# Gate logits of a routed expert layer from 32-column float32 tiles, once per unit of two head pairs

## The chip, the cores and the metric

The kernel runs on one core of a Trainium2 chip. The metric is the device time of one execution in microseconds (us); the time before is the median of three runs. The engines are TensorE (PE in the profile, PEld for its weight loads), VectorE (DVE), ScalarE (ACT), GpSimd (POOL) and SyncE (SP, which issues most DMA transfers).

## The reference

Sigmoid attention over 8 batches, 12 heads, 448 tokens and 64 elements a head, and behind it a layer of 8 experts of which each token uses one:

```python
scores = scale * np.matmul(q, k.transpose(0, 1, 3, 2)) - np.log(S)
attn = 1.0 / (1.0 + np.exp(-scores))
x = np.matmul(attn, v)                     # heads side by side: (8 * 448, 768)
logits = x @ w_gate                        # (3584, 8)
expert_idx = np.argmax(logits, axis=1)
probs = softmax(logits)                    # with 1e-09 under the line
gate_w = probs[np.arange(N), expert_idx]
for e in range(E):                         # xe: the tokens of expert e
    out[mask] = gate_w[mask, None] * (np.maximum(xe @ w1[e], 0.0) @ w2[e])
```

The gate's logits are a small product: 768 inputs and 8 outputs for each token. They decide which expert's weights are loaded, so they stand between the attention of a batch and its expert products.

## The kernel before

**Tiles.** A pair is two heads of one batch (128 rows); there are 48 pairs, 6 to a batch, and a unit is two pairs, so a batch has three units. A unit's attention runs in seven steps. `scores` (line 534) makes the score products of a step in the four 64x64 quarters of TensorE, `squash` (line 521) takes the sigmoid on ScalarE into a tile `at` of a ring of eight, and `weighted` (line 548) multiplies by the values into PSUM, `av`. All of this is in float32, of which each product shows as two records in the profile.

**When a unit's last values are made** (from line 551), ScalarE writes the product rounded to float32r, `xh` (line 556), VectorE writes the rest, `xl` (line 557), and `token_block` transposes the pair on VectorE into `xt` (line 411), which goes out to the table of tokens. The expert products of `moe` (lines 218 and 237) read `xh` and `xl`: each product is made from three float32r products, high by high, high by low and low by high, of 448 columns. `part_split` (lines 143 and 144) splits the weights in the same way, the high part on ScalarE and the low one on VectorE.

**The gate.** `gate_a` runs once per batch: twelve products (line 265), of `xh` and of `xl` of each pair, with `wgs`, the gate's weights as a high and a low half of eight columns each, add up in one PSUM tile of 16 rows; VectorE copies it into `g16`. `gate_b` turns `g16` into rows of tokens with four transpositions (line 274) and adds the halves. Then `gate_c`, `gate_d` and `gate_e` choose the experts, count the tokens and spread the gate weights.

**The order** is written by hand in `attention` (from line 576), a generator. Its step number is `s`, its unit `u` and the place in the unit `i`. Up to step 35 (`ALONE`) each step has one step of scores and, two steps back, one of values; behind that the seven steps of a unit run as one block at `i` = 6. From step 36 (`START`) the generator hands out 7 expert products at each of its two yields. Between the yields stand the loads and turns of the next unit's k and q (`READY`) and one piece of the gate of the batch whose last unit is done. On each engine the instructions run in the order in which they are written. So there is a lead-in with attention alone, in which the first batch's gate lies, then a long stretch in which expert products and blocks of attention take turns, then a last stage for the tokens that were not sent to their batch's most frequent expert (lines 677 to the end; `few_rows`, line 903, works in tiles of 32 columns, and `split_rows`, line 800, transposes 128x128 blocks).

Of the kernel before, what the change touches and what calls it, by code (L numbers as in the profile page):

```python
# [10 lines left out]
F32 = mybir.dt.float32  # L11
F32R = mybir.dt.float32r
# [4 lines left out]
ALU = mybir.AluOpType  # L17
AX = mybir.AxisListType

P = 128  # L20
NCH = 4
# [4 lines left out]
def tile_sigmoid_attention_top1_moe(  # L26
# [18 lines left out]
    nc = tc.nc  # L45
    B, H, S, D = q.shape
    NT, DM = out.shape
    E = w_gate.shape[1]
    DF = w1.shape[2]
    NP = H // 2  # L50
# [47 lines left out]
    base = const.tile([P, E], F32, name="base")  # L98
    nc.vector.memset(base, 0.0)
    gates = const.tile([P, B, NCH], F32, name="gates")  # L100
    g16 = const.tile([2 * E, NCH * P], F32, name="g16")
    nc.gpsimd.memset(g16, 0.0)

    wgs = const.tile([P, KD, 2 * E], F32R, name="wgs")

    wg = const.tile([P, KD, E], F32, name="wg")

    def setup():
        nc.gpsimd.tensor_copy(wgs[:, :, 0:E], wg)
        nc.gpsimd.tensor_sub(wgs[:, :, E : 2 * E], wg, wgs[:, :, 0:E].bitcast(F32))  # L110
        blank = wpool.tile([P, 1024], U32, tag="wst", bufs=RAWS_AHEAD, name="blank")
        blank3 = blank[:, : E * NT // P * 2].rearrange("p (r w) -> p r w", w=2)
        for w, val in enumerate((int(BIG), 0)):
            nc.gpsimd.iota(blank3[:, :, w], pattern=[[0, E * NT // P]], base=val, channel_multiplier=0)
        nc.gpsimd.dma_start(recs.rearrange("(p r) w -> p r w", p=P), blank3)
# [142 lines left out]
    xch = {}  # L258
    regs = {}

    def gate_a(b):
        psg = small_ps(b, "psg")
        for t in range(KD):
            for n in range(2):
                nc.tensor.matmul(  # L265
                    psg[: 2 * E, :S], wgs[:, t], xch[b, t][n],
                    start=(t == 0 and n == 0), stop=(t == KD - 1 and n == 1),
                )
        nc.vector.tensor_copy(g16[:, :S], psg[: 2 * E, :S])

    def gate_b(b):
        pl = small_ps(b, "pl")
        for c in range(NCH):
            nc.tensor.transpose(  # L274
                pl[:, c * 2 * E : (c + 1) * 2 * E], g16[:, c * P : (c + 1) * P], ident[: 2 * E, : 2 * E]
            )
        plv = pl[:, : NCH * 2 * E].rearrange("p (c n e) -> p c n e", n=2, e=E)
        sh = [P, NCH, E]

        def tl(nm, shape=sh, dt=F32):  # L280
# [3 lines left out]
            return a.unsqueeze(2).broadcast_to(sh)  # L284

        lg = tl("lg")
        nc.vector.tensor_copy(lg, plv[:, :, 0])
        nc.vector.tensor_add(lg, lg, plv[:, :, 1])
        mx = tl("mx", [P, NCH])
        nc.vector.tensor_reduce(mx, lg, axis=AX.X, op=ALU.max)  # L290
        eq = tl("eq")
# [132 lines left out]
    def small_ps(b, name):  # L424

        return ps_sc.tile([P, 512], F32, tag="sc", name=f"{name}_{b}")
# [84 lines left out]
        for _ in range(n):  # L511
            nc.tensor.matmul(ps[:, :P], ones, ones, start=True, stop=True)

    ats, psv = {}, {}

    ST = KC
    N_ST = NG // 2 * ST
# [20 lines left out]
    def weighted(s):  # L538
# [12 lines left out]
        if c == KC - 1:  # L551
            for g in two:
                pv = psv.pop(g)
                xh = xpool.tile([P, S], F32R, tag="xh", name=f"xh_{g}")
                xl = xpool.tile([P, S], F32R, tag="xl", name=f"xl_{g}")
                nc.scalar.copy(xh, pv[:, :S])  # L556
                nc.vector.tensor_sub(xl, pv[:, :S], xh.bitcast(F32))  # L557
                token_block(g, pv[:, :S])
                xch[divmod(g, NP)] = (xh, xl)
# [16 lines left out]
    def attention():  # L576
# [36 lines left out]
        for s in range(N_ST + 11):  # L613
# [11 lines left out]
            yield s, MIX[0]  # L625
            if i in READY and s < N_ST:
                READY[i](u)
            gb = s - PB
            if gb >= 0:
                b, r = divmod(gb, PB)  # L630
                r -= 3 if b == 0 else 2
                at = ("a", "b", None, "c", "l", None) + (("d", None, "e") if b else (None,) * 3 + ("d", "e"))
                what = at[r] if 0 <= r < len(at) else None
                if what == "a":
                    gate_a(b)
                elif what == "b":
                    pend_gate = gate_b(b)
                elif what == "c":
                    pend_gate = gate_c(b, *pend_gate)
# [418 lines left out]
```

## Time and profile before

| | us |
|---|---|
| time, median of 3 runs | 831.76 (830.7 to 833.89) |
| time of the profiled execution | 831.49 |
| its span, first to last instruction | 829.8 |
| TensorE products of line 265, busy | 21.0 in 8 stretches of 2.6 |
| transpositions of line 274, busy | 3.3 |
| copies of psg (line 269), busy on VectorE | 4.9 |

The profile comes from one execution. A timeline row is: start, length, engine, line, operation, output<-inputs by the kernel's names, the part of the array that a product uses (rows*columns), its sizes, how many merged records, and in brackets the idle time of the engine before it with what ended it. A row of a group has the count, then busy time and mean length in ns, then idle time before. TensorE's products are pipelined: one begins before the one ahead of it has ended, so the distance of two starts is what a product costs, and the length of a record is longer than that.

### The profile page before, as it was taken

To read this page: it belongs to the slowest core of one execution; us is meant where nothing else is said; L and a number is where in the kernel's file an instruction comes from. 1 tells how busy PE (TensorE), PEld (TensorE's weight loads), DVE (VectorE), ACT (ScalarE), POOL (GpSimd) and SP (SyncE) were. 2 spreads that over 40 slices of the span, in tenths; PEclk is the share of its full clock that TensorE was granted. 3 is DMA by queue.
4 is the path that set the end of the run, shared out by engine and by line. 5 is a ranking of instruction groups with operands and counts; after the bars stand their busy time and mean duration, and the time that the engine had idled before them with its cause. 6 is when DMAs were issued, how large, how long until landed. Compare 5 with 4: busy or idle time off the path is not lost.

```text
span 829.8 us, 15348 instructions
## 1 busy us (share of the span) xinstructions
PE 814.9 (98%) x5659; PEld 623.4 (75%) x5659; DVE 398.9 (48%) x851; ACT 383.7 (46%) x672; POOL 144.3 (17%) x214
## 2 busy tenths in 40 slices
PE   9999999999999999999999999999999999999994
PEld 6546677687697686786776876876867868999992
DVE  2446365353473264453562534733654535745650
ACT  5766635535534535446344445255363452233440
POOL 3426101210041000410021100400015001512201
PEclk9999999999999999999999999999999999999998
DMA  9999783684575763954758846647635432767921
GB/s 149 141 181 179 203 195 88 142 181 115 138 152 119 180 135 84 211 134 103 169 109 135 202 96 135 154 102 179 126 105 138 134 79 66 185 179 259 325 75 37
DMA packets 290929, 120.70 MB, mean 145 GB/s; under 512 B 204290, under 2 KB 283029, under 8 KB 290848
## 3 DMA queue, kind: packets, MB, share of 16 engines
q1 hardware_dynamic: 279856, 99.27, 52.1%
q0 software_dynamic: 8816, 19.46, 9.4%
q10 hardware_dynamic: 2176, 0.92, 0.8%
q8 instruction: 48, 0.79, 0.4%
q14 instruction: 33, 0.27, 0.1%
HBM read 97.55 MB, written 23.17 MB: 145 GB/s over the span
## 4 chain that ended last, share of the span: by engine, by line
PE 94%; DMA 2%; SPq 2%; issue 1%; POOL 0%; POOLq 0%; DVE 0%; DVEq 0%
PE ps L237 29%; PE ps L218 29%; PE sc L534 15%; PE av L548 14%; PE psg L265 2%; PE ps L881 2%; PE ps L861 2%; SPq L457 1%; DMA kn<-in_k_dram 1%; DMA qn<-in_q_dram 1%; DMA first<-in_k_dram 1%; DMA out_dram<-xo,rec_c 0%; PE pl L274 0%; SPq L497 0%; SPq L471 0%
## 5 line engine op out<-in xcount | busy, mean ns | idle before, releaser
L521 ACT ACTIVATE at<-sc,bias_s 128x448 f32<-128x448 f32 x336 | 196.2, 632 | 135.5 <-PE sc L534 134.3
L534 PE MATMUL sc<-qt,kt 64*64 64x448 f32 x1344 | 175.1, 545 | 1.9 <-DVE qt L505 1.8
L548 PE MATMUL av<-at,vn 64*64 64x448 f32 x1344 | 173.9, 537 | 0.0
L237 PE MATMUL ps<-hh,w2l 128*128 128x448 f32 x384 | 142.1, 370 | 0.0
L253 POOL DMA_DIRECT2D out_dram<-ob x96 | 61.5, 653 | 461.6 <-DVE ob L248 384.6
L237 PE MATMUL ps<-hh,w2h 128*128 128x448 f32 x384 | 141.6, 369 | 0.0
L218 PE MATMUL ps<-xl,w1h 128*128 128x448 f32 x384 | 141.5, 368 | 0.0
L218 PE MATMUL ps<-xh,w1l 128*128 128x448 f32 x384 | 140.9, 367 | 0.0
L237 PE MATMUL ps<-hl,w2h 128*128 128x448 f32 x384 | 140.8, 367 | 0.0
L218 PE MATMUL ps<-xh,w1h 128*128 128x448 f32 x384 | 140.5, 366 | 0.0
L557 DVE TENSOR_TENSOR xl<-av,xh 128x448 fp32r<-128x448 f32 x48 | 29.0, 604 | 216.6 <-ACT xh L556 216.6
L534 PEld LDWEIGHTS sc<-qt,kt 64*64 64x64 f32 x1344 | 79.9, 191 | 60.5 <-issue 25.9
L223 ACT ACTIVATE hh<-ps 128x448 fp32r<-128x448 f32 x64 | 35.0, 547 | 161.8 <-PE ps L218 161.7
L548 PEld LDWEIGHTS av<-at,vn 64*64 64x64 f32 x1344 | 64.0, 132 | 60.2 <-ACT at L521 25.5
L143 ACT CAST w2h<-wst 128x512 fp32r<-128x512 f32 x96 | 61.6, 659 | 87.0 <-PE ps L237 80.4
L218 PEld LDWEIGHTS ps<-xl,w1h 128*128 128x128 f32 x384 | 72.1, 188 | 11.0 <-issue 5.2
L237 PEld LDWEIGHTS ps<-hh,w2h 128*128 128x128 f32 x384 | 72.2, 188 | 9.5 <-issue 4.2
L237 PEld LDWEIGHTS ps<-hh,w2l 128*128 128x128 f32 x384 | 72.2, 188 | 8.4 <-issue 2.8
L218 PEld LDWEIGHTS ps<-xh,w1l 128*128 128x128 f32 x384 | 72.1, 188 | 8.4 <-issue 1.4
L218 PEld LDWEIGHTS ps<-xh,w1h 128*128 128x128 f32 x384 | 72.1, 188 | 6.6 <-ACT at L521 0.7
L237 PEld LDWEIGHTS ps<-hl,w2h 128*128 128x128 f32 x384 | 72.2, 188 | 5.6
L144 DVE TENSOR_TENSOR w2l<-wst,w2h 128x512 fp32r<-128x512 f32 x96 | 64.0, 683 | 22.7 <-ACT w2h L143 21.1
(164 smaller groups left out, 741.6 us busy)
## 6 DMA issues: line engine op xcount, KB each, us to landing
wst<-in_moe_w_dram SPq DMA_DIRECT2D x48, 512.0 KB, 4.5
wst<-in_moe_w_dram SPq DMA_DIRECT2D x56, 384.0 KB, 4.3
x_tok<-xt SPq DMA_DIRECT2D x64, 168.0 KB, 4.2
out_dram<-ob POOLq DMA_DIRECT2D x96, 112.0 KB, 3.2
kn<-in_k_dram SPq DMA_DIRECT2D x184, 56.0 KB, 4.1
qn<-in_q_dram SPq DMA_DIRECT2D x168, 56.0 KB, 3.1
vn<-in_v_dram SPq DMA_DIRECT2D x68, 112.0 KB, 3.8
raw<-in_moe_w_dram SPq DMA_DIRECT2D x12, 512.0 KB, 6.6
```

Source lines behind the costliest of these rows:

```text
L143: nc.scalar.copy(hi, st)
L144: eng.tensor_tensor(lo, st, hi.bitcast(F32), op=ALU.subtract)
L218: nc.tensor.matmul(ps[:, :S], a[:, ws], b_, start=(t == 0 and n == 0), stop=(t == KD - 1 and n == 2))
L223: nc.scalar.activation(hh[:, :S], ps[:, :S], AF.Relu)
L237: nc.tensor.matmul(ps[:, :S], a, b_, start=(j == 0 and n == 0), stop=(j == KF - 1 and n == 2))
L253: nc.gpsimd.dma_start(out[b * S : (b + 1) * S, cols].rearrange("(j r) f -> r j f", r=32), obv[32 * i : 32 * (i + 1)])
L265: nc.tensor.matmul(psg[: 2 * E, :S], wgs[:, t], xch[b, t][n], start=(t == 0 and n == 0), stop=(t == KD - 1 and n == 1),)
L521: nc.scalar.activation(at, ps[:, :S], AF.Sigmoid, bias=bias_s, scale=SCALE)
L534: nc.tensor.matmul(ps[quarter(g, h), :S], ks, ops[g, "q"][OWN[h]], start=True, stop=True)
L548: nc.tensor.matmul(psv[g][OWN[h], :S], ops[g, "v"][rows, c, :], at[rows], start=(c == 0), stop=(c == KC - 1))
L557: nc.vector.tensor_sub(xl, pv[:, :S], xh.bitcast(F32))
L861: nc.tensor.matmul(pss[j], a[:, js], b_, start=(t == 0 and m == 0), stop=(t == KD - 1 and m == 2))
```

## The change

The gate no longer reads `xh` and `xl`. A third copy of each pair's product, `plain`, is kept in float32 in the ring of `at`; VectorE writes it up to step 34, ahead of `xl`, and ScalarE behind it, after `xh`. `gate_unit` runs once per unit, on the unit before, at `i` = 2 between the two yields. It makes four float32 products of 32 columns and 256 tokens, one for each pair and each half of the tokens (tokens 0 to 255 and 192 to 447), each into 32 PSUM rows of its own. The weights are `wgp`: eight columns and 24 of zeros. VectorE copies the first unit's tile into `gsum` and adds the other two. `gate_b` then transposes four blocks of 128x128, and one reduction adds the two pairs' parts. `gate_a` is gone, with its twelve products and its copy.

```diff
-    g16 = const.tile([2 * E, NCH * P], F32, name="g16")
-    nc.gpsimd.memset(g16, 0.0)
-
-    wgs = const.tile([P, KD, 2 * E], F32R, name="wgs")
+    GC, GW = 32, 2 * P
+    gsum = const.tile([P, GW + P // 2], F32, name="gsum")
+    nc.gpsimd.memset(gsum, 0.0)
+
+    wgp = const.tile([P, KD, GC], F32, name="wgp")
+    nc.gpsimd.memset(wgp, 0.0)
...
-        nc.gpsimd.tensor_copy(wgs[:, :, 0:E], wg)
-        nc.gpsimd.tensor_sub(wgs[:, :, E : 2 * E], wg, wgs[:, :, 0:E].bitcast(F32))
+        nc.gpsimd.tensor_copy(wgp[:, :, 0:E], wg)
...
-    def gate_a(b):
-        psg = small_ps(b, "psg")
-        for t in range(KD):
-            for n in range(2):
-                nc.tensor.matmul(
-                    psg[: 2 * E, :S], wgs[:, t], xch[b, t][n],
-                    start=(t == 0 and n == 0), stop=(t == KD - 1 and n == 1),
-                )
-        nc.vector.tensor_copy(g16[:, :S], psg[: 2 * E, :S])
+    def gate_unit(u):
+
+        b, n = divmod(2 * u, NP)
+        psg = small_ps(u, "psg")
+        for m in range(2):
+            x = plain.pop(2 * u + m)
+            for half, at in enumerate((0, S - GW)):
+                rows = slice((2 * m + half) * GC, (2 * m + half + 1) * GC)
+                nc.tensor.matmul(psg[rows, :GW], wgp[:, n + m], x[:, at : at + GW], start=True, stop=True)
+        if n == 0:
+            nc.vector.tensor_copy(gsum[:, :GW], psg[:, :GW])
+        else:
+            nc.vector.tensor_add(gsum[:, :GW], psg[:, :GW], gsum[:, :GW])
 
     def gate_b(b):
         pl = small_ps(b, "pl")
-        for c in range(NCH):
-            nc.tensor.transpose(
-                pl[:, c * 2 * E : (c + 1) * 2 * E], g16[:, c * P : (c + 1) * P], ident[: 2 * E, : 2 * E]
-            )
-        plv = pl[:, : NCH * 2 * E].rearrange("p (c n e) -> p c n e", n=2, e=E)
+        for c, at in enumerate((0, P, 2 * P - (S - GW), 3 * P - (S - GW))):
+            to = c * P - c // 2 * GC
+            nc.tensor.transpose(pl[:, to : to + P], gsum[:, at : at + P], ident)
+        plv = pl.rearrange("p (c n x) -> p c x n", c=NCH, n=2)[:, :, :E]
...
-        nc.vector.tensor_copy(lg, plv[:, :, 0])
-        nc.vector.tensor_add(lg, lg, plv[:, :, 1])
+        nc.vector.tensor_reduce(lg, plv, axis=AX.X, op=ALU.add)
...
+                plain[g] = apool.tile([P, S], F32, tag="at", bufs=8, name=f"plain_{g}")
+                if s < ALONE:
+                    nc.vector.tensor_copy(plain[g], pv[:, :S])
                 nc.scalar.copy(xh, pv[:, :S])
+                if s >= ALONE:
+                    nc.scalar.copy(plain[g], pv[:, :S])
                 nc.vector.tensor_sub(xl, pv[:, :S], xh.bitcast(F32))
                 token_block(g, pv[:, :S])
...
+            if i == 2 and 0 < u <= NG // 2:
+                gate_unit(u - 1)
...
-                at = ("a", "b", None, "c", "l", None) + (("d", None, "e") if b else (None,) * 3 + ("d", "e"))
+                at = (None, "b", None, "c", "l", None) + (("d", None, "e") if b else (None,) * 3 + ("d", "e"))
                 what = at[r] if 0 <= r < len(at) else None
-                if what == "a":
-                    gate_a(b)
-                elif what == "b":
+                if what == "b":
```

On TensorE, in the mixed stretch, the gate of batch 1 stood before in the middle of the expert products of one weight tile (`ps_0_6`, the experts' first layer); the numbers behind the names only tell tiles apart:

```order
L218 MATMUL ps_0_6_1504<-xl_594,w1h_6_1415 128x448
L265 MATMUL psg_1520<-xh_967,wgs 16x448
L265 MATMUL psg_1520<-xl_968,wgs 16x448
L265 MATMUL psg_1520<-xh_973,wgs 16x448
L265 MATMUL psg_1520<-xl_974,wgs 16x448
L265 MATMUL psg_1520<-xh_1134,wgs 16x448
L265 MATMUL psg_1520<-xl_1135,wgs 16x448
L265 MATMUL psg_1520<-xh_1139,wgs 16x448
L265 MATMUL psg_1520<-xl_1140,wgs 16x448
L265 MATMUL psg_1520<-xh_1393,wgs 16x448
L265 MATMUL psg_1520<-xl_1394,wgs 16x448
L265 MATMUL psg_1520<-xh_1398,wgs 16x448
```

At the same place the change has one unit's four products (two rows that stand for two each):

```order
L219 MATMUL ps_0_6_1543<-xh_605,w1h_6_1454 128x448
L219 MATMUL ps_0_6_1543<-xl_606,w1h_6_1454 128x448
L270 MATMUL psg_1559<-plain_1430,wgp 32x256 x2
L270 MATMUL psg_1559<-plain_1437,wgp 32x256 x2
L219 MATMUL ps_0_6_1543<-xh_605,w1l_6_1455 128x448
```

The twelfth old product (of `xl_1399`) and the rest of the weight tile follow behind the first of these pieces. The other two units of the batch have places of their own, 7 and 14 steps earlier, and the transpositions stay one step behind the last unit's place.

On VectorE, in the lead-in, the work on the fourth unit's two pairs (`av_766` and `av_769` before, `av_790` and `av_793` in the change) reads before:

```order
L505 STREAM_TRANSPOSE kt_921<-kn_713 128x448
L557 TENSOR_TENSOR xl_968<-av_766,xh_967 128x448
L411 STREAM_TRANSPOSE xt_0_971<-av_766 128x14x32
L557 TENSOR_TENSOR xl_974<-av_769,xh_973 128x448
L411 STREAM_TRANSPOSE xt_0_971<-av_769 128x14x32
L505 STREAM_TRANSPOSE qt_978<-qn_718 128x448
L505 STREAM_TRANSPOSE kt_1017<-kn_788 128x448
```

and in the change:

```order
L508 STREAM_TRANSPOSE kt_936<-kn_733 128x448
L561 COPY plain_984<-av_790 128x448
L565 TENSOR_TENSOR xl_983<-av_790,xh_982 128x448
L414 STREAM_TRANSPOSE xt_0_988<-av_790 128x14x32
L561 COPY plain_992<-av_793 128x448
L565 TENSOR_TENSOR xl_991<-av_793,xh_990 128x448
L414 STREAM_TRANSPOSE xt_0_988<-av_793 128x14x32
L508 STREAM_TRANSPOSE qt_997<-qn_738 128x448
L272 COPY gsum<-psg_1020 128x256
L508 STREAM_TRANSPOSE kt_1042<-kn_818 128x448
```

Each pair has one copy more, ahead of its `xl`, and the copy into `gsum` stands between the turns of q and k. On TensorE the same unit's products come one step (scores and values) behind the last values of its pairs:

```order
L551 MATMUL av_790<-at_6_886,vn_615 64x448 x2
L551 MATMUL av_793<-at_6_888,vn_686 64x448 x2
L537 MATMUL sc_2_1004<-qt_771,kt_731 64x448 x2
L537 MATMUL sc_2_1005<-qt_842,kt_816 64x448 x2
L551 MATMUL av_1014<-at_0_928,vn_773 64x448 x2
L551 MATMUL av_1017<-at_0_930,vn_844 64x448 x2
L270 MATMUL psg_1020<-plain_984,wgp 32x256 x2
L270 MATMUL psg_1020<-plain_992,wgp 32x256 x2
L537 MATMUL sc_3_1028<-qt_771,kt_731 64x448 x2
```

Nothing stood there before: the values of `av` were followed by the next step's scores.

On VectorE at the start of the mixed stretch, the split of the experts' second weight tile (`w1l_1`) stood before behind four operations of the fifth unit and one turn:

```order
L144 TENSOR_TENSOR w1l_0_1113<-wst_0_951,w1h_0_1112 128x768
L557 TENSOR_TENSOR xl_1135<-av_995,xh_1134 128x448
L411 STREAM_TRANSPOSE xt_0_971<-av_995 128x14x32
L557 TENSOR_TENSOR xl_1140<-av_998,xh_1139 128x448
L411 STREAM_TRANSPOSE xt_1_1143<-av_998 128x14x32
L505 STREAM_TRANSPOSE kt_1145<-kn_923 128x448
L144 TENSOR_TENSOR w1l_1_1158<-wst_1_983,w1h_1_1157 128x768
```

and stands now behind six and the turn:

```order
L145 TENSOR_TENSOR w1l_0_1138<-wst_0_966,w1h_0_1137 128x768
L561 COPY plain_1161<-av_1014 128x448
L565 TENSOR_TENSOR xl_1160<-av_1014,xh_1159 128x448
L414 STREAM_TRANSPOSE xt_0_988<-av_1014 128x14x32
L561 COPY plain_1168<-av_1017 128x448
L565 TENSOR_TENSOR xl_1167<-av_1017,xh_1166 128x448
L414 STREAM_TRANSPOSE xt_1_1172<-av_1017 128x14x32
L508 STREAM_TRANSPOSE kt_1174<-kn_938 128x448
L145 TENSOR_TENSOR w1l_1_1187<-wst_1_1002,w1h_1_1186 128x768
```

More of the change, by code (lines that the diff above doesn't have):

```diff
@@ L512, in warm_up @@
             nc.tensor.matmul(ps[:, :P], ones, ones, start=True, stop=True)
-    ats, psv = {}, {}
+    ats, psv, plain = {}, {}, {}
     ST = KC
```

## The prediction

> **What bounds the kernel now.** I read the engines' busy times, the chain of waits, then the timeline of TensorE around the old gate products. The first shows which engine is full, the second whether its time sets the end.
>
> ```profile
> PE 814.9 (98%) x5659; PEld 623.4 (75%) x5659; DVE 398.9 (48%) x851; ACT 383.7 (46%) x672; POOL 144.3 (17%) x214
> PE 94%; DMA 2%; SPq 2%; issue 1%; POOL 0%; POOLq 0%; DVE 0%; DVEq 0%
> ```
>
> TensorE is busy 98% of the span and holds 94% of the chain. VectorE and ScalarE are half idle. So from where the loads stop setting the pace, a microsecond of TensorE time is a microsecond of the kernel, and work on the other two costs something only where TensorE has to wait for it. The change must be priced on TensorE, in two stretches: the lead-in, where attention runs alone, and the long mixed stretch behind it, from the experts' first product on.
>
> **What goes in the mixed stretch.** The old products and transposes of batch 1 stand among the experts' products:
>
> ```profile
> 108.41 0.36 PE L265 MATMUL psg<-xh,wgs 128*16 128x448 f32 x1
> ...
> 110.86 0.37 PE L218 MATMUL ps<-xh,w1l 128*128 128x448 f32 x1
> 113.50 0.37 PE L218 MATMUL ps<-xh,w1h 128*128 128x448 f32 x1
> 113.80 0.42 PE L274 MATMUL pl<-ident,g 16*128 16x16 f32 x4
> ...
> 114.45 0.36 PE L218 MATMUL ps<-xh,w1l 128*128 128x448 f32 x1
> ```
>
> Twelve products take 110.86 - 108.41 = 2.45 us, 0.204 each, the same step as the experts' own; they come and go without a gap. The four transposes cost 114.45 - 113.50 less two ordinary steps (0.41): 0.54 us. Seven batches (1 to 7) lie in this stretch: **-7 x 2.45 = -17.15 us**.
>
> **What comes there.** Twenty of the 24 units (the fifth on) fall into it, each with four 128*32 products of 256 columns between experts' products. The kernel's end has products of exactly this shape, and the way back to full-width products is seen behind a block of 64*64 attention:
>
> ```profile
> L903 PE MATMUL few<-kept,x_few 128*32 128x256 f32 x48 | 2.8, 381 | 0.0
> 811.46 0.28 PE L881 MATMUL ps<-w2l_r,hr 128*128 128x256 f32 x1
> 811.59 0.28 PE L881 MATMUL ps<-w2h_r,hr 128*128 128x256 f32 x1
> 811.80 2.80 PE L903 MATMUL few<-kept,x_few 128*32 128x256 f32 x48
> 131.45 0.95 PE L548 MATMUL av<-at,vn 64*64 64x448 f32 x8
> 132.33 0.47 PE L237 MATMUL ps<-hh,w2h 128*128 128x448 f32 x1
> 132.64 0.37 PE L237 MATMUL ps<-hl,w2h 128*128 128x448 f32 x1
> ```
>
> The 48 records are 24 float32 products, two records each (six tokens' blocks by four tiles). Four run side by side: 12 groups in 2.80 us, the last one 0.38 long, so (2.80 - 0.38) / 11 = 0.22 us a group. A unit is four products, eight records, two groups: 0.44. Going in costs 0.21 against an ordinary step of 0.13 (811.46 to 811.59): 0.08 to 0.09. Coming back: eight 64*64 records take 0.75 (the prologue's rows below step by that), so the next product was due at 132.20 and began at 132.33 (0.13), and the one behind it came after 0.31 in place of 0.20 (0.11). A visit is 0.44 + 0.09 + 0.24 = 0.77 us: **20 x 0.77 = +15.4**.
>
> That way in and out speaks against the change, and the Trainium skill has a rule on it (TensorEngine Tiling (Array Packing), Key Properties): a change of the tiling mode drains TensorE. The rows agree that a change costs something, 0.33 us a visit. A full drain at both ends would make it more, which is the first rival below; with no cost at all a visit would be 0.44 and the 20 would be 6.6 us cheaper.
>
> The new transposes are 128x128, as the final stage has them:
>
> ```profile
> 761.65 0.36 PE L237 MATMUL ps<-hl,w2h 128*128 128x448 f32 x1
> 761.85 0.60 PE L800 MATMUL px<-ident,xo 128*128 128x128 f32 x4
> ...
> 762.49 0.37 PE L237 MATMUL ps<-hh,w2h 128*128 128x448 f32 x1
> ```
>
> Four cost 762.49 - 761.65 - 0.41 = 0.43 us, less than the narrow ones: **7 x (0.43 - 0.54) = -0.8**. The mixed stretch sums to **-2.5 us**.
>
> **The copies on ScalarE and VectorE there.** ScalarE copies each pair's product a second time (about half of the 0.97 us of two casts, see the row of 98.60 below). I cost this at nothing: TensorE comes to the unit 49 products (seven yields, 10.0 us) after the block. What follows the block on ScalarE shifts by about 0.9 us, and the tightest place is the sixth weight tile:
>
> ```profile
> 101.84 1.80 DVE L144 TENSOR_TENSOR w1l<-wst,w1h 128x768 fp32r<-128x768 f32 x2
> 98.60 0.97 ACT L556 CAST xh<-av 128x448 fp32r<-128x448 f32 x2
> 99.87 1.60 ACT L143 CAST w1h<-wst 128x768 fp32r<-128x768 f32 x2
> ```
>
> VectorE first works off its own four operations of the two pairs and takes up w1l at 101.84, while the first of the two casts from 99.87 on, 1.60 us together, ends near 100.7; 0.9 us later it is still in time. Without that cover each late tile would cost up to 0.9 us. The sums into gsum (256 wide) and one reduction for two small operations hide in VectorE's idle half.
>
> **The lead-in.** Here the old gate of batch 0 disappears:
>
> ```profile
> 49.97 0.95 PE L548 MATMUL av<-at,vn 64*64 64x448 f32 x4
> 50.85 0.37 PE L265 MATMUL psg<-xh,wgs 128*16 128x448 f32 x1
> ...
> 54.25 0.93 PE L548 MATMUL av<-at,vn 64*64 64x448 f32 x8
> 55.11 0.42 PE L274 MATMUL pl<-ident,g 16*128 16x16 f32 x4
> 56.32 0.93 PE L548 MATMUL av<-at,vn 64*64 64x448 f32 x8
> ```
>
> From 49.97 + 0.75 to 54.25 - 0.75: **-2.78 us**, of which 0.34 is the way in and out. The transposes cost 56.32 - 0.75 - 55.00 = 0.57; wide ones would be 0.43 + 0.34 = 0.77: **+0.2**.
>
> Four units fall here, and they **wait**. As the rows of the change show, a unit's products stand one step (scores and values, 1.5 us) behind the last values of that unit, while VectorE makes plain of the first pair, then xl and xt, and only then plain of the second. Around the fourth unit the trace of before has
>
> ```profile
> 61.18 0.93 PE L548 MATMUL av<-at,vn 64*64 64x448 f32 x8
> 61.93 0.93 PE L534 MATMUL sc<-qt,kt 64*64 64x448 f32 x8
> 62.68 0.93 PE L548 MATMUL av<-at,vn 64*64 64x448 f32 x8
> 61.70 0.65 DVE L505 STREAM_TRANSPOSE kt<-kn 128x448 f32<-128x448 f32 x1
> 63.07 0.62 DVE L557 TENSOR_TENSOR xl<-av,xh 128x448 fp32r<-128x448 f32 x1 [0.72 <-ACT xh L556]
> 63.61 0.64 DVE L411 STREAM_TRANSPOSE xt<-av 128x448 f32<-128x448 f32 x1
> 64.17 0.58 DVE L557 TENSOR_TENSOR xl<-av,xh 128x448 fp32r<-128x448 f32 x1
> L269 DVE COPY g<-psg 16x448 f32<-16x448 f32 x8 | 4.9, 612 | 16.9 <-PE psg L265 16.9
> ```
>
> The values end at 62.11. A copy of 448 elements a row takes 0.61. The first fits into the 0.72 us in which VectorE waited for ScalarE's cast, so xl still starts at 63.07; the second takes the place of the xl at 64.17 and ends at 64.78. TensorE stands ready at 62.68 + 0.75 + 0.13 = 63.56: it waits about 1.25 us, with the semaphore 1.3. Queued behind it are the next scores, so ScalarE's sigmoids and all that follows slip too. The bounds are 0 (the copy would have to be 0.6 faster and xl out of the way) and 1.9 (another 0.6 behind a late transposition). I take 1.3, which comes out of the rows. VectorE in turn waits for the unit's products before gsum; behind it stand the turns of the next k and q, wanted only at the next unit's first scores, four steps (6 us) later, so that wait costs nothing. A unit here costs 0.44 + 0.34 + 1.3 = 2.1 us.
>
> The first unit is mostly paid already:
>
> ```profile
> 31.75 0.54 PE L534 MATMUL sc<-qt,kt 64*64 64x448 f32 x2
> 34.11 0.65 PE L534 MATMUL sc<-qt,kt 64*64 64x448 f32 x2 [1.81 <-DVE qt L505]
> ```
>
> TensorE idles here behind a load of q, 34.11 - 31.75 - 0.38 = 2.0 us: the first unit's place lies a few steps ahead of it, so its 2.1 us shrink to 0.1. The other three: 3 x 2.1 = 6.2 (from 0.78 + 1.3): **+6.3** with the first.
>
> The fifth unit's copies lie on VectorE at the start of the experts:
>
> ```profile
> 73.39 0.62 DVE L557 TENSOR_TENSOR xl<-av,xh 128x448 fp32r<-128x448 f32 x1 [1.19 <-ACT xh L556]
> 76.09 0.92 DVE L144 TENSOR_TENSOR w1l<-wst,w1h 128x768 fp32r<-128x768 f32 x1
> 76.68 0.36 PE L218 MATMUL ps<-xl,w1h 128*128 128x448 f32 x1
> 77.06 0.47 PE L218 MATMUL ps<-xh,w1l 128*128 128x448 f32 x1
> ```
>
> TensorE already waits for w1l there (0.38 where a step is 0.20). One copy fits into the 1.19 us of idle time, the other pushes w1l by 0.55: **+0.55**. The lead-in sums to -2.78 + 0.2 + 6.3 + 0.55 = **+4.3 us**.
>
> **The sum.** -2.5 + 4.3 = +1.8 us on the profiled execution's 831.49 us: **833.3 us**. That execution lies 0.27 below the median of the runs shown, 831.76, so it stands for them. A measurement of this kernel can tell some 0.5% (4.2 us) from no change, and +1.8 is inside.
>
> **Rivals.**
> *A full drain at each change of shape (slower).* Price: an experts' record is 0.37 long against a step of 0.20 (0.16 to drain going in), a narrow one 0.38 against 0.22 (0.16 coming out), and a full-width weight load, the mean of the next row, would stand open for its 0.19.
>
> ```profile
> L218 PEld LDWEIGHTS ps<-xh,w1h 128*128 128x128 f32 x384 | 72.1, 188 | 6.6 <-ACT at L521 0.7
> ```
>
> That is 0.51 in place of 0.33 a visit: 23 visits x 0.18 = 4.1 more, **837.4 us**. It decides from 0.43 a visit on (2.4 more in sum, past 0.5%). The rows of 811.80 and 132.33 speak against it; that no row shows a 128*32 group directly followed by full width speaks for it. Chance 0.15, with ScalarE's late casts, which would end on the same side.
> *Cheap visits and no wait (faster).* If the switches cost 0.1 a visit (-5.3) and VectorE were early enough to save half the waits (-2), the time is **826 us**. The idle VectorE speaks for it, the two rows of the switches against. Chance 0.07.
> *Four tiles do the work in a quarter.* The old products were 16 columns wide; were tiles to cut their time by four, 7 x 2.45 would become 4.3 us and with the lead-in unchanged at +4.3 the end is 831.5 - 12.9 - 0.8 + 4.3 = **822 us**. The group's own step, 0.22 for a record of 256 columns in float32 (two records a product) against 0.20 for 448 columns before, speaks against it. The Trainium skill (TensorEngine Tiling, Theoretical Speedup) gives up to four times for 32 columns or fewer; the trace does show four side by side, but float32 takes the gain back. Chance 0.03.
> *The tiles don't overlap*, and the change does not do what it says: eight records of 0.22 in a row, 1.3 us more in each of 23 visits, some **864 us**. Line 903 shows the overlap. Chance 0.02.
> My forecast has 0.73.
>
> **Chances and range.** The forecast's own bounds: the wait 0 to 1.9 for three units (-3.9 to +1.8), and the visit 0.6 to 0.95 for twenty (-3.4 to +3.6). Both ends at once are unlikely; 828.5 to 837.5 leaves out about 2 in 10 and takes in the full drain. Faster by over 0.5%: 0.11 (the two faster rivals and a tail of the forecast); within it: 0.70; slower: 0.19 (the drain, no overlap and the other tail).
>
> **What would show it.** In the new trace: a unit's eight records in about 0.6 us (0.22 + 0.38) and the experts' next steps 0.77 late in sum; gaps of about 1.3 us on TensorE before the second pair's products at three places between 38 and 67 us, released by VectorE's plain; the wait at the second weight tile near 0.7; the transposes at 0.43. It is wrong if ScalarE's copies show up as waits for w1l or w2l behind the blocks, if the first unit moves the 34.11 us start, or if the switches cost other than 0.33.

## The result and the profile after

| | before | changed |
|---|---|---|
| time, us, median | 831.1 (829.78 to 833.89) | 838.7 (837.61 to 840.14) |
| ratio | 1 | 1.0086, 95% interval 1.0072 to 1.01 |
| span of the profiled run, us | 829.8 | 836.5 |

The change makes the kernel slower by 0.9%: 7.6 us where 1.8 were forecast, and 838.7 lies outside the range of 828.5 to 837.5. The engines' busy times hardly tell it. TensorE is still full, and the other two are a little busier with the copies:

```profile
PE 819.5 (98%) x5755; PEld 627.6 (75%) x5755; DVE 407.8 (49%) x869; ACT 400.2 (48%) x710; POOL 143.0 (17%) x214
PE 94%; DVE 2%; issue 1%; DMA 1%; ACT 1%; POOL 0%; POOLq 0%; DVEq 0%
```

The second line is the chain of waits: VectorE had 0% of it before and has 2% now, ScalarE 1%. To see where the time went, I took the starts of the same TensorE instructions in both traces, each counted from the first attention score, and subtracted (the middle column gives the starts in the trace of before, from the start of the span). From the 101st product on, over four fifths of the span, the change gives 3 us back:

| TensorE comes to | before, us | changed minus before, us |
|---|---|---|
| the fifth unit's first scores | 58.81 | +2.00 |
| the experts' first product | 72.72 | +4.99 |
| their 25th product | 77.97 | +8.31 |
| their 101st product | 104.55 | +9.92 |
| the last product of the last expert | 776.95 | +6.95 |
| the end | 829.76 | +7.16 |

**The mixed stretch is as forecast.** A visit in the rows of TensorE (start, duration, line, output and inputs, count):

```profile
181.99 0.37 PE L219 MATMUL ps<-xh,w1l 128*128 128x448 f32 x1
182.29 0.64 PE L270 MATMUL psg<-plain,wgp 128*32 128x256 f32 x8
182.86 0.47 PE L219 MATMUL ps<-xh,w1h 128*128 128x448 f32 x1
183.17 0.36 PE L219 MATMUL ps<-xl,w1h 128*128 128x448 f32 x1
```

From 181.99 to 183.17 are 1.18 us where two ordinary steps take 0.41: the visit costs 0.77, as forecast. All 20 measured in this way sum to 15.6 us (0.77 to 0.78 each, one 0.95), the old products to 17.27, and the seven groups of wide transposes cost 0.44 each where the narrow ones cost 0.54. That is -2.4 us, forecast -2.5.

**The lead-in is not.** Around the fourth unit, at the place that the prediction looked at, ScalarE before shows two casts in one go and the sigmoids behind them:

```profile
62.50 0.97 ACT L556 CAST xh<-av 128x448 fp32r<-128x448 f32 x2
63.34 2.28 ACT L521 ACTIVATE at<-sc,bias_s 128x448 f32<-128x448 f32 x4
```

VectorE, ScalarE and TensorE now show (in brackets the idle time before a row and what ended it):

```profile
63.84 0.59 DVE L561 COPY plain<-av 128x448 f32<-128x448 f32 x1
65.03 0.62 DVE L565 TENSOR_TENSOR xl<-av,xh 128x448 fp32r<-128x448 f32 x1 [0.60 <-ACT xh L562]
65.57 0.64 DVE L414 STREAM_TRANSPOSE xt<-av 128x448 f32<-128x448 f32 x1
66.13 0.58 DVE L561 COPY plain<-av 128x448 f32<-128x448 f32 x1
64.46 0.53 ACT L562 CAST xh<-av 128x448 fp32r<-128x448 f32 x1 [0.29 <-DVE plain L561]
66.75 0.53 ACT L562 CAST xh<-av 128x448 fp32r<-128x448 f32 x1 [1.76 <-DVE plain L561]
67.18 2.46 ACT L524 ACTIVATE at<-sc,bias_s 128x448 f32<-128x448 f32 x4
65.10 0.62 PE L270 MATMUL psg<-plain,wgp 128*32 128x256 f32 x4
66.77 0.62 PE L270 MATMUL psg<-plain,wgp 128*32 128x256 f32 x4 [1.04 <-DVE plain L561]
```

Read the casts first. ScalarE's xh does not start beside VectorE's plain: it waits for it, though both only read av. Before, xh waited for nothing of VectorE's, and both casts ran one behind the other. Now a unit's eight operations stand in one file over two engines: plain, xh, xl, xt, and again. The second cast starts 2.29 us behind the first, and the sigmoids of the next attention steps stand behind it in ScalarE's queue (four at 67.18). TensorE's wait for plain is there as forecast. The view of waits below has only 2.3 us of it in four places, but that counts the idle time behind modelled ends of records; by the starts of the scores, each of the second to fourth units loses 2.30 to 2.44 us at its visit, where 2.1 were forecast.

**The start of the experts is the worst place.** The fifth unit's copies stand ahead of the second weight tile there, and the view of waits and TensorE's rows show:

```profile
PE psg L270 <- DVE plain L561: 2.3, 4, 1.0
PE ps L219 <- DVE w1l L145: 1.2, 1, 1.2
PE ps L219 <- ACT w1h L144: 0.6, 1, 0.6
...
80.56 0.53 ACT L562 CAST xh<-av 128x448 fp32r<-128x448 f32 x1 [1.75 <-DVE plain L561]
80.99 0.83 ACT L144 CAST w1h<-wst 128x768 fp32r<-128x768 f32 x1
81.13 0.62 DVE L565 TENSOR_TENSOR xl<-av,xh 128x448 fp32r<-128x448 f32 x1 [0.60 <-ACT xh L562]
82.76 0.92 DVE L145 TENSOR_TENSOR w1l<-wst,w1h 128x768 fp32r<-128x768 f32 x1
80.88 0.37 PE L219 MATMUL ps<-xh,w1l 128*128 128x448 f32 x1
81.88 0.47 PE L219 MATMUL ps<-xh,w1h 128*128 128x448 f32 x1 [0.63 <-ACT w1h L144]
82.19 0.37 PE L219 MATMUL ps<-xl,w1h 128*128 128x448 f32 x1
83.73 0.47 PE L219 MATMUL ps<-xh,w1l 128*128 128x448 f32 x1 [1.17 <-DVE w1l L145]
```

The late second cast makes w1h late, which stands behind it on ScalarE. It makes VectorE's second xl late too, and behind that stand its transposition, a turn and w1l; the two copies are two operations more ahead of w1l than before (w1h itself had ended at 81.82). TensorE shows steps of 1.00 and 1.54 us where an ordinary one is 0.20, 2.13 us lost where before lost 0.17. Behind them the granted clock falls, as the busy times by stretch show (span, busy of PE, PEld, DVE, ACT, POOL with counts, then the granted clock, the DMA share and GB/s):

```profile
77.00:84.00 7.00, 5.19 (x25) 3.78 (x21) 5.19 (x9) 3.06 (x6) 6.39 (x8) 1.00 0.62 94
85.00:88.40 3.40, 3.40 (x11) 2.99 (x11) 1.49 (x3) 0.00 (x0) 1.12 (x3) 0.51 1.08 348
```

Between 84.70 and 88.40 ten products step by 0.37 instead of 0.20, 1.65 us more. The parts between the experts' first and 101st products sum up: waits 2.13 - 0.17, the visit 0.77, the clock 1.65, and 0.47 of late w1l behind the next block make 4.85 of the 4.93 in the table (9.92 - 4.99). The 0.47 has the same root on the other side: xl, which does not read plain, waits there for ScalarE's plain on the same av, and what stands behind xl on VectorE comes later.

```profile
108.60 0.62 DVE L565 TENSOR_TENSOR xl<-av,xh 128x448 fp32r<-128x448 f32 x1 [13.09 <-ACT plain L564]
```

The theory to test, A: the loss comes from the copies, because two engines that read one av stand behind one another, which delays the casts and what is queued behind them. Its rival B: the loss comes from the visits on TensorE. Every ratio below is to the kernel before, run on the same chip.

### The profile page after: what moved, and what is told of

Its sections match the earlier page's. It is cut to its first block, busy times and chain, and to the rows that moved or that the text cites. A ratio compares the mean times of both kernels' runs of the same rounds, so it can differ in the third digit from the quotient of the medians.

```text
span 836.5 us, 15619 instructions
## 1 busy us (share of the span) xinstructions
PE 819.5 (98%) x5755; PEld 627.6 (75%) x5755; DVE 407.8 (49%) x869; ACT 400.2 (48%) x710; POOL 143.0 (17%) x214
## 4 chain that ended last, share of the span: by engine, by line
PE 94%; DVE 2%; issue 1%; DMA 1%; ACT 1%; POOL 0%; POOLq 0%; DVEq 0%
PE ps L238 29%; PE ps L219 28%; PE sc L537 15%; PE av L551 15%; PE ps L889 2%; PE ps L869 2%; PE psg L270 2%; PE ps_warm L515 1%; DVE plain L561 1%; DVE xt L414 0%; DMA out_dram<-xo,rec_c 0%; PE pl L280 0%; DVE xl L565 0%; ACT xh L562 0%; DMA x_tok<-xt 0%
## 5 line engine op out<-in xcount | busy, mean ns | idle before, releaser
L219 PE MATMUL ps<-xh,w1h 128*128 128x448 f32 x384 | 142.2, 370 | 0.7 <-ACT w1h L144 0.6
```

Source lines behind the costliest of these rows:

```text
L219: nc.tensor.matmul(ps[:, :S], a[:, ws], b_, start=(t == 0 and n == 0), stop=(t == KD - 1 and n == 2))
```

## The experiments

**Copies without the new gate.** The kernel before, its twelve products kept, with the change's copies alone:

```diff
+                plain[g] = apool.tile([P, S], F32, tag="at", bufs=8, name=f"plain_{g}")
+                if s < ALONE:
+                    nc.vector.tensor_copy(plain[g], pv[:, :S])
                 nc.scalar.copy(xh, pv[:, :S])
+                if s >= ALONE:
+                    nc.scalar.copy(plain[g], pv[:, :S])
```

> The kernel before (old twelve products a batch) with the change's copies into plain alone, which nothing reads. Theory A: the copies keep their harm at the experts' start (+3 to +4 us) and in the lead-in that of sigmoids queued behind late casts (0 to +1): 834.5 to 836 against 831.1. Theory B: the copies lie beside TensorE's work and cost nothing, 831.1 within 0.7.

Measured: 837.76 us against 830.13, ratio 1.0089 (1.0075 to 1.0102). The copies alone cost as much as the whole change, more than A had put on them, and B falls. TensorE's waits move from plain to the sigmoids, which shows that ScalarE's queue is what comes late:

```profile
PE sc L534 <- ACT at L521: 3.8, 3, 2.0
PE ps L218 <- DVE w1l L144: 1.2, 1, 1.2
```

**The same copies in another order.** In the lead-in VectorE makes plain behind xl and xt, not ahead of xh:

```diff
-                if s < ALONE:
-                    nc.vector.tensor_copy(plain[g], pv[:, :S])
                 nc.scalar.copy(xh, pv[:, :S])
...
                 token_block(g, pv[:, :S])
+                if s < ALONE:
+                    nc.vector.tensor_copy(plain[g], pv[:, :S])
```

> The run with the copies alone, but in the lead-in VectorE makes plain behind xl and xt, so that xh no longer stands behind it. Theory A1 (the harm is that ScalarE's cast waits for VectorE's copy and the sigmoids behind it come late): the lead-in's +4.6 falls to 1.5 or less, sum 831.5 to 834. Theory A2 (it is the 0.6 us a copy on VectorE, that makes turns and w1l late): the lead-in stays at +4 or more, sum 836 to 838.

Measured: 831.88 against 830.92, 1.0013 (1.0001 to 1.0025). The copies are the same in number, kind and engine, and 6.7 of 7.6 us are gone. ScalarE's rows at the fourth unit, first of the run before this one, then of this one:

```profile
65.59 0.53 ACT L559 CAST xh<-av 128x448 fp32r<-128x448 f32 x1 [0.29 <-DVE plain L558]
67.88 0.53 ACT L559 CAST xh<-av 128x448 fp32r<-128x448 f32 x1 [1.76 <-DVE plain L558]
68.31 2.21 ACT L521 ACTIVATE at<-sc,bias_s 128x448 f32<-128x448 f32 x4
```

```profile
61.67 0.97 ACT L557 CAST xh<-av 128x448 fp32r<-128x448 f32 x2
62.50 1.19 ACT L521 ACTIVATE at<-sc,bias_s 128x448 f32<-128x448 f32 x2
```

The sigmoids start 0.83 us behind the first cast instead of 2.72. At the experts' first product this run stands 0.97 us ahead of before, the other 4.61 behind it. Nor is it the ring of `at`: plain takes its buffers there in both runs. The copy's own time on VectorE (0.6 us) is nearly free in the lead-in, but not at the second weight tile: it still waits 1.07 us for w1l. So of the 1.96 us of waits at the experts' start about half is the two copies' own time ahead of w1l, and not their order.

The Trainium skill (PSUM — Partial Sum Buffer, Terms) says that two engines must not access one bank of PSUM at once, and that reads against reads count. The rows shown agree with it: a reader of an av begins when the other engine's reader ahead of it in the code has ended. The wait is one for a semaphore, which the program as built contains; what the chip would do without it, no run shows.

**The fifth unit alone.** In the changed kernel, ScalarE makes its two copies just ahead of its visit, behind the casts of the weights:

```diff
+                if s == FIFTH:
+                    late.append((g, pv))
...
+                while late:
+                    g, pv = late.pop(0)
+                    nc.scalar.copy(plain[g], pv[:, :S])
                 gate_unit(u - 1)
```

> The changed kernel, with one thing undone at the experts' start: the fifth unit's two copies into plain are made by ScalarE just ahead of its four products, not by VectorE ahead of the casts. Theory A (two engines that read one av stand behind one another, so the late casts make w1h and w1l late, TensorE idles 2.5 us in two pieces and its clock then falls to half for some 3.5 us): both waits of the first expert shrink to the 0.4 us of before, no stretch at a clock of 0.5, and 3 to 4 us less than the changed kernel's 838.7: about 835.2. Theory B (the visits are dear, the start of the experts is not what costs): within 0.7 us of 838.7.

Measured: 835.7 against 830.13, 1.0067 (1.0053 to 1.008). Both waits for weights are gone and the clock stays at 1.00, but a new wait takes part of the gain:

```profile
82.88 1.06 PE L270 MATMUL psg<-plain,wgp 128*32 128x256 f32 x8 [0.95 <-ACT plain L642]
```

By the ratios it is 0.2% (1.6 us) less than the changed kernel, half of what A expected, and not clear of the noise: the changed kernel run a second time, below, has 1.0071. What the trace shows is that the two waits are gone and that the copy came too close ahead of its reader.

**Visits later.** The first four units' visits one step later, then the same with the order of the copies put right and the fifth unit's copies behind the second weight tile's split:

```diff
-            if i == 2 and 0 < u <= NG // 2:
+            if i == (3 if u <= 4 else 2) and 0 < u <= NG // 2:
                 gate_unit(u - 1)
```

and for the second, beside this and plain behind xt, the fifth unit's copies:

```diff
+            if s == START:
+                for g, pv in late:
+                    nc.vector.tensor_copy(plain[g], pv[:, :S])
```

> The changed kernel with the four products of the first four units one attention step (1.5 us) later. Theory A: the waits of TensorE for plain (2.3 us in four pieces) go, so up to 2.3 us less, about 836.5; the first expert's waits and the fallen clock stay, since the fifth unit is not touched. Theory B (visits dear): no change, since all 24 visits are still there: 838.7.

> The changed kernel, with plain still copied from av, but in the lead-in by VectorE behind xl and xt, the first four units' products a step later, and the fifth unit's copies behind the second weight tile's split. Theory A1 (order of the readers): the lead-in falls from +5 to within 2 us of before and the experts' start to within 0.5, so 830 to 832.5 beside 830.1 of before. Theory A2 (VectorE's extra 0.6 us a copy): 834 or more.

Measured: 1.0071 (1.0057 to 1.0084) and 1.0023 (1.0013 to 1.0034). In the first, TensorE's wait for plain is gone, but in its place it waits 2.6 us for sigmoids, since psg takes its buffer from the scores' ring and the sigmoids are late behind the casts:

```profile
PE psg L270 <- ACT at L524: 2.6, 3, 1.2
```

The second keeps waits of 1.9 us for the now later plain, so that its lead-in ends 2.92 us behind before where A1 allowed 2; by the ratio, 832.0 beside the 830.1 of the expectation, it lies in A1's range.

**Where plain comes from.** GpSimd makes plain as xh + xl from SBUF for every unit, so that it reads no av, and the first four units' visits are a step later, as in the runs above:

```diff
-                    nc.vector.tensor_copy(plain[g], pv[:, :S])
...
+                nc.gpsimd.tensor_add(plain[g], xh.bitcast(F32), xl.bitcast(F32))
```

> The changed kernel, with plain made by GpSimd as xh + xl from SBUF, so that nobody but xh, xl and xt reads av, as before the change; the first four units' products one step later. Theory A (the copies from av do the harm, the visits are worth 1 to 3 us): lead-in within 1 us of before, the experts' start as before, mixed stretch -1 to -2.5: 828 to 831 where before has 830.1. Theory B (it is the visits): still 6 us over before, 836. If GpSimd's sums hold up VectorE or its own loads, it comes out between.

Measured: 835.11 against 830.92, 1.0043 (1.0027 to 1.0059), between the two theories. The lead-in is only 1.3 us behind before, as A wants, but at the experts' start the two sums hold up VectorE's subtraction:

```profile
76.67 2.24 POOL L562 TENSOR_TENSOR plain<-xh,xl 128x448 f32<-128x448 f32 x2
76.76 2.98 DVE L145 TENSOR_TENSOR w1l<-wst,w1h 128x768 fp32r<-128x768 f32 x1
80.73 0.93 DVE L145 TENSOR_TENSOR w1l<-wst,w1h 128x768 fp32r<-128x768 f32 x1
```

The same subtraction takes 0.93 us without them and 2.98 beside them, and TensorE waits 2.0 us for it. Behind that wait the granted clock was 0.50 from 80.6 to 84.0 us, so this run too pays for a slower clock. The Trainium skill (SBUF — State Buffer, Who interferes with whom) says that a VectorE instruction with two inputs in SBUF is locked out while a GpSimd instruction reads SBUF. The rows fit such a lock: the sums end at 78.91, 0.93 later is 79.84, and the subtraction ended at 79.74.

**The price of a visit.** Two kernels, for rival B: every product from the fifth unit on twice in one visit, and a visit for each pair:

```diff
-        for m in range(2):
-            x = plain.pop(2 * u + m)
+        xs = [plain.pop(2 * u + m) for m in range(2)]
+        for m in (0, 1, 0, 1) if u >= 4 else (0, 1):
+            x = xs[m]
```

```diff
-                gate_unit(u - 1)
+                if u <= 4:
+                    gate_unit(u - 1)
+                else:
+                    gate_unit(u - 1, (0,))
+                    halves.append(u - 1)
```

> The changed kernel, with the four products of every unit from the fifth on issued twice in one visit (the second time over the same sums). Theory A (a visit costs 0.77: two groups of 0.22 and 0.33 of switching): 20 x 0.44 = 8.8 us more, 847.5. Theory B (a full drain at each switch, and tiles that hardly overlap): 20 x 0.9 to 1.7 = 18 us or more, 857 and over.

> The changed kernel, with each unit's four products from the fifth on in two visits, one for each pair, ten expert products apart. Each visit more costs one way in and out and no product. Theory A (0.33 a visit): 20 x 0.33 = 6.6 us more than the changed kernel, ratio to before about 1.0165; half of the pair's overlap of four tiles may be lost, up to 0.22 a visit, 4.4 more. Theory B (a full drain, 0.51): 10 us more, 1.021. No cost of the switch: no more than 1 us.

Measured: 844.22, 1.0177 (1.0164 to 1.0191), and 851.62, 1.0247 (1.0228 to 1.0265). In the first, a visit takes 1.20 us instead of 0.77, so the four products are 0.43 (forecast 0.44) and going in and out 0.34 (forecast 0.33). In the second the two halves stand three expert products apart (not ten, as the expectation has it), and each half visit takes 0.76 us, as much as a whole one:

```profile
182.71 0.63 PE L272 MATMUL psg<-plain,wgp 128*32 128x256 f32 x4
183.26 0.47 PE L219 MATMUL ps<-xh,w1h 128*128 128x448 f32 x1
183.57 0.37 PE L219 MATMUL ps<-xl,w1h 128*128 128x448 f32 x1
183.78 0.36 PE L219 MATMUL ps<-xh,w1l 128*128 128x448 f32 x1
184.07 0.63 PE L272 MATMUL psg<-plain,wgp 128*32 128x256 f32 x4
```

My expectation of 0.33, up to 0.55, a further visit was too low: four records on two tiles take as long as eight on four (0.63 and 0.64), so a half visit saves no product time at all. By TensorE's rows twenty further visits are some 15 us; by the ratios it is 13.4.

**The order, once more, in the changed kernel.** Since the order decided it with the copies alone, the changed kernel was run with that edit and nothing else:

> The changed kernel with only the order of the readers of av changed: in the lead-in VectorE makes plain behind xl and xt, so ScalarE's xh waits for TensorE alone; visits and their places as changed. Theory A1: of the 7.6 us of the copies alone, 6.4 were the order, so about 6 less than the changed kernel, less what the first four units now wait longer for plain (0.7 each, 2.8): 833 to 836, ratio 1.003 to 1.006. Theory A2 (the order matters only without the gate's visits): 838 to 839, ratio 1.0086.

Measured: 841.79 against 830.78, 1.0127 (1.0105 to 1.015). It is slower still, and both expectations fail. The visits stand where they stood, plain is made last, and so TensorE waits for it:

```profile
PE psg L270 <- DVE plain L566: 8.2, 8, 1.3
...
74.00:76.00 2.00, 2.00 (x16) 0.80 (x12) 0.54 (x2) 1.16 (x2) 0.00 (x0) 0.50 1.10 285
```

The second row is the stretch from 74 to 76 us, with the clock at 0.50 behind these waits; it had fallen once before, from 56.2 us on. So the order is good only where the visits are late enough for it. Two more runs complete the square: the visits of units 1, 2, 4 and 5 a further step later and the fifth unit's copies behind the second weight tile, with plain last and with plain first.

```diff
-            if i == (3 if u <= 4 else 2) and 0 < u <= NG // 2:
+            if 0 < u <= NG // 2 and i == {1: 4, 2: 4, 3: 3, 4: 4, 5: 3}.get(u, 2):
                 gate_unit(u - 1)
```

> The run with plain last, with the products of units 1, 2, 4 and 5 another step later, so that they no longer wait for plain. The 1.9 and 0.7 us of waits before psg shrink to 0.7: about 1.9 less than that run, ratio 1.000 (0.999 to 1.002).

> The run with the visits of the lead-in later still, but with the change's order of the readers in the lead-in (VectorE's plain ahead of ScalarE's xh); the fifth unit's copies stay behind the second weight tile. With the visits out of the way of plain, what differs from that run is the order alone. If the order does the harm by itself: 2 to 5 us more in the lead-in, ratio 1.004 to 1.008. If the order only mattered through what waits for it at the visits and at the experts' start: within 1 us of that run, ratio 1.001 to 1.003.

| ratio to before | plain first, as changed | plain last |
|---|---|---|
| visits as changed | 1.0086 (1.0072 to 1.01) | 1.0127 (1.0105 to 1.015) |
| visits later, fifth unit's copies late | 1.0041 (1.0027 to 1.0056) | 1.0016 (1.0004 to 1.0028) |

In the lower row the order is the only difference, and it is worth 0.25% (2.1 us), at the lower end of what was expected; the two intervals just touch. The trace has it in the lead-in: the experts' first product comes 5.69 us behind before with plain first, 1.89 with plain last. In the upper row it turns round. Neither cause stands alone: the change needs the copies behind the casts **and** the visits behind the copies.

**Visits beside the blocks of attention.** With the waits out of the way, 12 of the 20 visits were put directly ahead of a block of 64x64 attention, which changes TensorE's tiling anyway:

```diff
             elif i == ST - 1:
+                if u <= NG // 2 and beside(u):
+                    gate_unit(u - 1)
                 steps(s - ST + 2, ST, s + 1)
```

> The run before this one, with 12 of the 20 visits of the mixed stretch moved to stand directly ahead of a block of 64x64 attention, so that the way back to full width is the block's own. If a switch is paid only against full-width work (0.33 a visit): up to 12 x 0.33 = 4.0 less than that run, ratio 0.995. If 128x32 to 64x64 costs as much as any other change: one of two ends is saved, 12 x 0.09 to 0.24 = 1.1 to 2.9 less, ratio 0.997 to 0.999. If the switches cost nothing anywhere: no difference.

> The run with 12 visits beside the blocks, with the first unit's visit back at one step later (not two), where its sum does not stand behind a turn that waits for its load: the new wait of 1.8 us of the scores for gsum goes, about 1 less (part of it lies under the load of q), ratio 0.998.

> The run before this one, with all but the last of the visits of the mixed stretch directly ahead of a block (7 more of them), and the gate's transposes of batches 1 to 6 four steps later for it. At the 0.18 to 0.26 that a moved visit saved: 1.2 to 1.8 us less, ratio 0.996. If the later choice of the expert makes a batch's first weights late, it is slower instead, by waits for w1h at the start of a batch.

Measured: 830.36 us, 0.9993 (0.998 to 1.0006); 827.52, **0.9948 (0.9931 to 0.9966)**; and 832.99, 1.0021 (1.001 to 1.0033). A block takes 10.96 us by itself and 11.53 with a visit ahead of it (one of the twelve 11.75), so the visit costs 0.57 there instead of 0.77: 0.20 is saved, which is part of the way in and out of 0.34 and not all of it. The second run moves the first unit's visit back one step and is the fastest of all, faster than both kernels and than the 0.998 that was expected. Between the two the profiled spans differ by 0.7 us (826.5 and 825.8), less than the medians do (2.8), so what that one step is worth is not settled.

The second run's busy times show what the new gate is worth where nothing waits for it, TensorE busy 2.8 us less than before (814.9):

```profile
PE 812.1 (98%) x5755; PEld 620.7 (75%) x5755; DVE 407.2 (49%) x869; ACT 398.6 (48%) x710; POOL 143.6 (17%) x214
```

The third run goes too far. To have the last visit of a batch beside a block, it chooses the experts of six batches four steps later, and at 535 us the next batch's weights and VectorE's ob are late, and behind TensorE's wait the granted clock was 0.50 from 539.8 to 543.2 us:

```profile
534.53 0.96 DVE L145 TENSOR_TENSOR w1l<-wst,w1h 128x768 fp32r<-128x768 f32 x1 [3.06 <-ACT w1h L144]
537.32 0.64 DVE L247 STREAM_TRANSPOSE ob<-ps 128x448 f32<-128x448 f32 x1
538.11 0.44 PE L219 MATMUL ps<-xh,w1h 128*128 128x448 f32 x1 [2.35 <-DVE ob L247]
```

**The changed kernel again.**

> The changed kernel once more, beside the others on one chip. Ratio 1.0086. Theory A (its clock fell at the experts' start because TensorE stood idle for 2.5 us there): the fall to half is there again and the first expert loses 1 to 2 us by it. If the runs with the same waits (copies alone, products twice) are the rule: no fall, the two waits alone.

Measured: 837.17 against 830.78, 1.0071 (1.0054 to 1.0088), with the fall of the clock (0.56 between 85.0 and 88.4 us). The run with every product twice has nearly the same waits there, and no fall:

```profile
81.56 0.47 PE L219 MATMUL ps<-xh,w1h 128*128 128x448 f32 x1 [0.40 <-ACT w1h L144]
83.41 0.47 PE L219 MATMUL ps<-xh,w1l 128*128 128x448 f32 x1 [1.18 <-DVE w1l L145]
...
85.00:88.40 3.40, 3.40 (x17) 3.10 (x17) 1.16 (x3) 0.19 (x1) 1.64 (x3) 1.00 1.03 309
```

So the waits don't always bring the fall, and what decides it stays open.

## Why the prediction was wrong

- **The step that failed** is "The first fits into the 0.72 us in which VectorE waited for ScalarE's cast, so xl still starts at 63.07", and with it "One copy fits into the 1.19 us of idle time". Both take it that VectorE can read av while ScalarE reads it. The runs showed that the second reader waits for the first: of these 0.72 and 1.19 us the first cast itself took 0.53 and 0.54 on the same av, and a copy put there pushes the cast. At the fourth unit xl began 0.40 us later than the forecast has it (65.03 where 63.07, moved by the 1.56 between the two traces, is 64.63), and the second plain, for which TensorE waits, ended 0.37 later (66.71). In the copies alone, undoing this order gave back 6.7 of 7.6 us.
- **The lead-in** was put at +3.7 without the fifth unit and measured +4.99. By the starts of the scores the second to fourth units lose 2.30 to 2.44 us each (forecast 2.1), the old gate gives back 3.3 (forecast 2.8), the new transposes cost 0.7 (forecast 0.2), and 0.55 more comes at the last step. ScalarE's sigmoids behind the late casts, which the prediction named only in passing, fall into the same places: with the copies alone the second and the fourth unit lose 1.45 and 1.49 us there without any visit. The prediction asked who is queued behind TensorE's and VectorE's new waits, and saw no new wait on ScalarE at all.
- **The fifth unit** was put at +0.55. It cost 1.96 us of waits and, in the changed kernel's profile, 1.65 of a slower clock, for which the sum had no term; the start of the experts is the largest part of the miss. About half of the waits is the order. The other half is both copies' own time ahead of w1l, which stays with the order undone (1.07). The wait at the second weight tile, said to be near 0.7, was 1.00 and 1.54 at two products.
- **Right in mechanism and size:** the visit (0.77), the way in and out (0.34 for 0.33), the group's 0.22, the wide transposes (0.44 for 0.43), and the mixed stretch in sum (-2.4 for -2.5). The copies on ScalarE there were put at nothing and cost 0.47 at one block (0.38 and 0.49 us steps behind 111 us), and nothing that the table shows behind it. The first unit's cost did vanish under the load of q.
- **The rivals:** the full drain would have given 837.4 and is not it, since the runs price the switch at 0.34; a time near a rival's is no sign of its mechanism. ScalarE's late casts had been set down beside the drain without a price, and they were the main cause, in the lead-in and at the start of the experts, not behind the later blocks.

What stays open: how the lead-in's +4.99 divides between waits for plain and for sigmoids, since the two fall into the same places and taking one away grows the other (the square above), and when the clock falls.

## What to carry to other kernels

Idle time of an engine in front of a shared buffer is not free time if the engine it waits for is using that buffer: put a new reader behind the readers that others wait for, then move its own consumer behind it, and check both, because here the order alone made the changed kernel slower. Price a moved or added operation on every engine whose queue it touches, the half-idle ones too, where a pipeline starts up and nothing is buffered yet. A small product in another tiling costs its way in and out, and is cheapest where the tiling changes anyway, as long as nothing that starts a load moves with it.

## What the runs showed of the hardware

- In no run do two engines' readers of the same av, a PSUM tile, overlap. In the changed kernel's trace plain and xh of one av stand 0.03 us apart in the lead-in, whichever is ahead in the code begins first, and the second comes a copy (0.6 us) later. These are semaphore waits of the program as built.
- Behind two gaps, of 1.00 and 1.54 us from product to product, the granted clock was 0.51 for about 3.4 us; it fell in both profiles of the changed kernel and not in others with the same waits (copies alone, products twice, two visits). It fell behind other waits as well: with GpSimd's sums, twice with the order alone, and with nearly all visits beside blocks, each time for 3.4 us. The Trainium skill (TensorE: Matmul & The Clock Gate, What's actually happening) gives a free-running window of about 3.4 us that must be idle for the clock to be halved. The length of the slow stretch agrees with it and a free-running window would explain the chance; but TensorE was not idle for 3.4 us on end here.
- With tiles of 32 columns side by side, four cost no more than two: eight float32 records on four tiles took 0.64 us, four on two tiles 0.63.
- A subtraction of VectorE from SBUF took 2.98 us instead of 0.93 beside two sums of GpSimd, which took 1.16 and 1.13.
